# LayerNorm by pairs of batches, merged stores of the gate, earlier fetches for the mixing stage and an x store on two queues, in a fused delta-rule, gMLP and channel-mix kernel

## The chip, the cores and the metric

The kernel runs on one core of a Trainium2 chip. Its engines are TensorE (PE, with its weight loads as PEld), VectorE (DVE), ScalarE (ACT), GpSimd (POOL) and SyncE (SP), and each works through its own instructions in order. DMAs are issued here by SP and POOL, and after the change by ACT as well. The metric is the device time of one execution in microseconds (us). Three runs before the change took 823.33, 824.58 and 827.2 us.

## The reference

Three layers follow each other; 4 batches of 768 tokens, 8 heads of 48 features.

```python
k_n = k / (norm(k) + 1e-6)                       # layer 1: delta rule, token by token
for t in range(768):
    y[t]  = q[t] @ state
    state = state + beta[t] * outer(k_n[t], v[t] - k_n[t] @ state)
x = y with its heads side by side                # (4, 768, 384)

h = gelu_tanh(x @ w_in)                          # layer 2: gMLP, 1024 wide
u, v = h[..., :512], h[..., 512:]
v_n = (v - mean(v)) / sqrt(var(v) + 1e-6) * g_ln # over the 512 features
v_s = einsum('ts,bsd->btd', w_sg, v_n) + b_sg    # mixes all 768 tokens
x   = x + (u * v_s) @ w_out

xk, xr = blends of x and the x of the token before    # layer 3: channel mix
out = sigmoid(xr @ w_r) * (relu(xk @ w_k) ** 2 @ w_v)
```

All is float32; large products are made of three passes over values split in a high and a low part.

## The kernel before, in words

**The loop.** The tokens are cut into 12 steps of 64 (names with `s`); two steps are a group (`g`, 0 to 5). The 32 pairs of batch and head are handled in two halves `o`: batches 0 and 1, batches 2 and 3. Each step and half runs six stages (`st_rq`, `st_d0`, `st_l`, `st_d1`, `st_s`, `st_y`), the two halves three stages apart. PE's matmuls of a stage need the residual `r` that DVE makes (L426), and DVE's `r` needs the PE matmuls before it (L458, L488). For group g+1 DVE meanwhile inverts the triangular blocks (`solver`, L328 to L413, which ends with the transposed `DT` of L411).

**Layer 2 beside it.** When a group's x is done, `store_x` (L538) copies it by 8 DMAs for each half into `xT`; `x_split` (L558) makes its high and low part (`xh`, `xl`), and the products with `w_in` are put as *units* between the stages on PE: `v_units` (L588) for one batch each, `u_units` (L639) for two batches. `v_end` (L600) takes gelu of a v into one of four buffers `v`; `ln_steps` (L608) takes its statistics on DVE, and once the last batch is there, 4 small POOL operations (L622 to L625) make scale and shift for all four batches; `apply` (L628) then normalises each v in place on ACT and stores it to DRAM (`vn_d`, L634). A `v` buffer is free for the next group when that store has landed. In the last group the four operations are done for two batches at a time.

**Jobs.** The weights `w_out` and `w_k` come as float64 and are narrowed to high and low parts by jobs (`narrow`, L144): a load `raw`, ACT (L154), four DVE operations (L159 to L165), POOL (L167), ACT (L110), POOL (L113), and two stores (`put`, L192). `tick` (L789) starts jobs; from tick `LATE` on more of them.

**The order of the work.** In this stage the code is recorded in the order of `run`, `tick`, `fill` and `background` for PE, ACT, DVE and POOL, and their instructions stay in it. SP's instructions are placed by a scheduler.

**After the loop.** Lines 836 to 880 finish the last group's units and prepare the mixing with `w_sg`: `load_ws` loads a block of it (`wst`) and splits it into `ws0h`, `ws0l` or `ws1h`, `ws1l`; `load_v` loads a normalised v (`vst`) and splits it (`vh`, `vl`). `mix` and `project` (L923, L940) are layer 2's second half, `shift` and the last loop (L995 to L1044) layer 3.

Of the kernel before, what the change touches and what calls it, by code (L numbers as in the profile page):

```python
# [7 lines left out]
F32 = mybir.dt.float32  # L8
# [8 lines left out]
B, H, S, D = 4, 8, 768, 48  # L17
DM = 384
FF = 1024
HF = 512  # L20
P = 128
C = 64
NG = 6
# [13 lines left out]
RUN = (3, 1, 2)  # L37
SUMS = (0,)
EVERY = 12
LATE = 116  # L40
JLAG = 1
BUDGET = 1.4
UNITS = 6.1
GSTEP = 2
JS = 18
NT_ = (3, 3, 3)
LNW = 2
LAGX = 7
LAGU = 2
SHARE = ((1, 4, 1), (1, 3, 1), (2, 5, 1))  # L50
NRAW = 3
# [25 lines left out]
def fused_kernel(  # L77
# [17 lines left out]
    nc = tc.nc  # L95
    V, A, G, T = nc.vector, nc.scalar, nc.gpsimd, nc.tensor

    cp = ctx.enter_context(tc.tile_pool(name="cp", bufs=1))
    dp = ctx.enter_context(tc.tile_pool(name="dp", bufs=1, space=bass.MemoryType.DRAM))
    stg = ctx.enter_context(tc.tile_pool(name="stg", bufs=2))  # L100

    xT = cp.tile([P, B, 3, S + 1], F32, name="xT")
# [4 lines left out]
    def split(eng_hi, eng_lo, src, hi, lo):  # L107

        if eng_hi is A:
            A.activation(hi, src, AF.Copy)  # L110
        else:
            eng_hi.tensor_scalar(hi, src, 1.0, None, op0=ALU.mult)
        eng_lo.tensor_tensor(lo, src, hi.bitcast(F32), op=ALU.subtract)  # L113
# [69 lines left out]
    def scratch(dram, name, nblk, n, cw=CW, pool=stg):  # L183

        hi = dp.tile([nblk, P, n], F32, name=name + "_dh")
        lo = dp.tile([nblk, P, n], F32, name=name + "_dl")

        def job(i, j):
            parts = []
            yield from narrow(dram, i, j, None, None, cw, pool, parts=parts)  # L190

            def put():  # L192
                for d, x in zip((hi, lo), parts):
                    nc.sync.dma_start(out=d[i, :, j:j + cw], in_=x.bitcast(F32))

            yield 0, put

        return hi, lo, [lambda i=i, j=j: job(i, j) for i in range(nblk) for j in range(0, n, cw)]

# [7 lines left out]


    vn_d = dp.tile([B, NG, P, HF], F32, name="vn_d")
    u_d = dp.tile([B, 4, P, S], F32, name="u_d")  # L210
    wo_dh, wo_dl, jobs = scratch(w_out, "wo", 4, DM, DM // 2)
    wk_dh, wk_dl, j1 = scratch(w_k, "wk", 3, FF)
    jobs += j1
# [4 lines left out]
    with ExitStack() as at:  # L218
# [319 lines left out]
        def store_x(g, o, yst):  # L538
            ts_ = slice(1 + P * g, 1 + P * g + P)
            for h in range(2):  # L540
                for i in range(2):
                    nc.sync.dma_start(out=xT[D * h:D * h + D, 2 * o + i, :, ts_],  # L542
                                      in_=yst[64 * h:64 * h + D, 4 * i:4 * i + 3, :])
            for h, e, n, blk, row in ((0, 0, 32, 0, 96), (0, 32, 16, 1, 96),
                                      (1, 0, 16, 1, 112), (1, 16, 32, 2, 96)):
                nc.sync.dma_start(out=xT[row:row + n, 2 * o:2 * o + 2, blk, ts_],  # L546
                                  in_=yst[64 * h + e:64 * h + e + n, 3:8:4, :])


# [57 lines left out]

        def ln_steps(g, b, v):  # L608
            mv, vs = vstat[g]
            n = 2 if g == NG - 1 else B  # L610
            st6 = fp.tile([P, 6], F32, name="st6")
            V.bn_stats(out=st6, in_=v)
            yield 0.6
            V.bn_aggr(out=mv[:, b], in_=st6)
            yield 0.1
            if b % n == n - 1:
                b0 = b + 1 - n
                var = fp.tile([P, n], F32, name=f"var{n}")
                yield 1, None
                rs = fp.tile([P, n], F32, name=f"rs{n}")  # L620
                nm = fp.tile([P, n], F32, name=f"nm{n}")
                G.tensor_scalar(var, mv[:, b0:b + 1, 1], EPS, None, op0=ALU.add)  # L622
                G.tensor_scalar(nm, mv[:, b0:b + 1, 0], -1.0, None, op0=ALU.mult)
                G.tensor_tensor(rs, var, nhalf[:, :n], op=ALU.pow)
                G.tensor_tensor(nm, nm, rs, op=ALU.mult)  # L625
                yield 2, None

                def apply(i):  # L628
                    A.activation(vs[b0 + i], vs[b0 + i], AF.Identity, bias=nm[:, i:i + 1],
                                 scale=rs[:, i:i + 1])  # L630
                    if (b0 + i, g) == (0, NG - 1):
                        to_ring(0, g, vs[0])
                    else:
                        nc.sync.dma_start(out=vn_d[b0 + i, g], in_=vs[b0 + i])  # L634

                for i in range(n):
                    yield LNW, lambda i=i: apply(i)

        def u_units(g, o, e, xh, xl):  # L639
            def mm(d, c, i, first, last):  # L640
                if first and d == 0:
                    vstat["u"] = bank()[:].rearrange("p a b -> p (a b)")
                w, a = ((wu_hi, xh), (wu_lo, xh), (wu_hi, xl), (wu_lo, xl))[i]
                ds_ = slice((2 * e + d) * P, (2 * e + d) * P + P)
                T.matmul(vstat["u"][:, 2 * P * d:2 * P * d + 2 * P], lhsT=w[:, c, ds_],  # L645
                         rhs=a[:, c].rearrange("p b t -> p (b t)"), start=first, stop=last)
                if last and d:
                    ug = fp.tile([P, 2, 2, P], F32, name="ug")
                    A.activation(ug.rearrange("p d b t -> p (d b t)"), vstat["u"],
                                 AF.Gelu_apprx_tanh)  # L650
                    for k in range(2):
                        nc.sync.dma_start(
                            out=u_d[2 * o:2 * o + 2, 2 * e + k, :, P * g:P * g + P].rearrange(
                                "b p t -> p b t"), in_=ug[:, k])

            return (g, o), lambda: (steps(0.5, lambda *a: mm(0, *a), 1)
                                    + steps(0.5, lambda *a: mm(1, *a), 1))
# [67 lines left out]
        running = []  # L725
        jobs = in_jobs + jobs
# [34 lines left out]
        k = 0  # L761
# [27 lines left out]
        def tick():  # L789
            g, n = divmod(point[0], 24)  # L790
            point[1] = min(g, 1) + 1
            gg, nn = divmod(point[0] - GRAM0, 24)
            if nn == 0 and 0 <= gg and gg + 2 < NG:
                grams.extend(gram(gg + 2))
            if n == 0 and g + 1 < NG:
                streams.append([point[0] + SOLVE0, solver(g + 1), "solve"])
            late = point[0] >= LATE
            if jobs and len(running) < RUN[1 + late] and n % (4 if late else EVERY) == 0:
                start_job(LJ5 if late else LJ)
            background(BUDGET * (B0 if g == 0 else 1))  # L800
            while len(jobs) > n_rest and len(running) < RUN[0]:
                start_job()
            if grams and (point[0] - GRAM0) % GSTEP == 0:
                for _, f in grams.pop(0):
                    f()
            point[0] += 1
# [16 lines left out]
        while opened[0]:  # L823
# [8 lines left out]
    vr = vx.enter_context(tc.tile_pool(name="vr", bufs=9, side="right", reuse_waits="tile"))  # L832
    banks[0] = ps
    ws = [[wq.tile([P, 6, DM], F32R, name=f"ws{t}{x}", tag=f"w{t}{x}") for x in ("h", "l")]
          for t in range(2)]
    b_sb = wq.tile([P, S], F32, name="b_sb")
    nc.sync.dma_start(out=b_sb, in_=b_sg.partition_broadcast(P))

    def load_ws(t, i):
        wst = vr.tile([P, DM], F32, name="wst", bufs=3)  # L840
        nc.sync.dma_start(out=wst, in_=w_sg[i * P:(i + 1) * P, t * DM:t * DM + DM])
        split(A, V, wst, ws[t][0][:, i], ws[t][1][:, i])

    ring = {}

# [2 lines left out]
    def fetch_v(b, c):  # L848
        vsts[b, c] = vr.tile([P, HF], F32, name="vst", bufs=3)
        nc.sync.dma_start(out=vsts[b, c], in_=vn_d[b, c])  # L850

    def load_v(b, c):
        if (b, c) not in vsts:
            fetch_v(b, c)
        to_ring(b, c, vsts.pop((b, c)))

    def to_ring(b, c, vst):
        vh = vr.tile([P, HF], F32R, name="vh")
        vl = vr.tile([P, HF], F32R, name="vl")
        split(A, G if c % 3 else V, vst, vh, vl)  # L860
        ring[b, c] = (vh, vl)
# [3 lines left out]
        ahead += [lambda i=i: load_ws(0, i), lambda i=i: load_v(0, i)]  # L865
    ahead.append(lambda: load_ws(0, 5))
    for c in range(3):
        fetch_v(0, c)
    ahead += [lambda i=i: load_ws(1, i) for i in range(6)]
    while later or splits or units or streams or opened[0]:  # L870
        background(2)
        units.sort(key=lambda u: (u[0][0], u[2]))
        fill(5)
        point[0] += 1
        if ahead:
            ahead.pop(0)()
# [31 lines left out]
    us, gs = {}, {}  # L908

    def load_u(b, t):  # L910
        us[b, t] = mp.tile([P, 4, DM], F32, name="u", bufs=3)
        nc.sync.dma_start(out=us[b, t],
                          in_=u_d[b, :, :, t * DM:t * DM + DM].rearrange("d p t -> p d t"))

    def mix_mm(pt, b, t, d, c):
        ds_ = slice(d * P, d * P + P)
# [189 lines left out]
```

## Time and profile before

| | |
|---|---|
| three runs | 823.33, 824.58, 827.2 us |
| the profiled execution | 823.41 us, of which the trace spans 821.7 us |
| busy: PE, DVE, ACT, POOL | 724.4, 526.6, 361.1, 192.1 us |
| granted TensorE clock, mean | 0.956 of full speed |
| DMA packets, bytes | 84969, 89.20 MB, mean 109 GB/s |

The loop lasts to about 385 us of the span, the transition to 416 us, the mixing and projecting to 567 us and layer 3 to the end. A busy PE is not PE at its peak: the granted clock has two levels, and in the page's row of clocks a 9 is full speed. A row of the timeline gives start, duration, engine, line, operation, tiles, and in brackets how long the engine was idle before it and what ended that. `SPq` is the instant at which SP's queue issues a DMA.

### The profile page before, as it was taken

To read this page: it belongs to the slowest core of one execution; us is meant where nothing else is said; L and a number is where in the kernel's file an instruction comes from. 1 tells how busy PE (TensorE), PEld (TensorE's weight loads), DVE (VectorE), ACT (ScalarE), POOL (GpSimd) and SP (SyncE) were. 2 spreads that over 40 slices of the span, in tenths; PEclk is the share of its full clock that TensorE was granted. 3 is DMA by queue.
4 is the path that set the end of the run, shared out by engine and by line. 5 is a ranking of instruction groups with operands and counts; after the bars stand their busy time and mean duration, and the time that the engine had idled before them with its cause. 6 is when DMAs were issued, how large, how long until landed. Compare 5 with 4: busy or idle time off the path is not lost.

```text
span 821.7 us, 23659 instructions
## 1 busy us (share of the span) xinstructions
PE 724.4 (88%) x10126; PEld 657.4 (80%) x10126; DVE 526.6 (64%) x1087; ACT 361.1 (44%) x732; POOL 192.1 (23%) x226
## 2 busy tenths in 40 slices
PE   3388898969969969697779979999999999999998
PEld 3345676857857867486679969999999999999998
DVE  6989689668668679134349596738945645653432
ACT  2234455535635634555443333205744534542431
POOL 3254233323313412424323535111000000000000
PEclk9989999979979979889979989999999999999999
DMA  8313343344444434534598755308400000000000
GB/s 235 81 52 99 85 127 111 97 145 116 105 134 124 110 108 120 155 117 116 175 316 276 241 201 182 108 0 259 107 30 20 10 30 20 16 24 21 19 20 29
DMA packets 84969, 89.20 MB, mean 109 GB/s; under 512 B 25856, under 2 KB 68992, under 8 KB 84864
## 3 DMA queue, kind: packets, MB, share of 16 engines
q1 hardware_dynamic: 80128, 78.64, 31.7%
q0 software_dynamic: 4736, 9.04, 3.9%
q8 instruction: 79, 1.29, 0.7%
q14 instruction: 26, 0.21, 0.1%
HBM read 56.86 MB, written 26.08 MB: 101 GB/s over the span
## 4 chain that ended last, share of the span: by engine, by line
PE 63%; DVE 11%; DMA 7%; SPq 5%; ACT 3%; issue 2%; POOL 1%; ACTq 0%; DVEq 0%; POOLq 0%
PE ms L141 34%; PE ms L920 8%; PE ms L645 4%; PE ms L593 3%; PE rk L434 3%; PE ms L522 3%; DVE tmp L325 2%; PE rk L488 2%; SPq L546 2%; DMA vn_d<-v 2%; SPq L542 2%; PE rk L458 2%; PE ms L686 2%; PE sps L508 1%; DMA wk_dh<-raw 1%
## 5 line engine op out<-in xcount | busy, mean ns | idle before, releaser
L426 DVE TENSOR_TENSOR r<-vk,rk 128x384 f32<-128x384 f32 x40 | 22.0, 551 | 83.4 <-PE rk L488 53.2
L167 POOL TENSOR_TENSOR na<-na,raw 128x256 int32<-128x256 int32 (+2 forms) x43 | 36.7, 853 | 126.2 <-DVE na L165 83.0
L141 PE MATMUL ms<-wvh,sh 128*128 128x384 f32 x192 | 64.9, 338 | 0.0
L141 PE MATMUL ms<-wvl,sh 128*128 128x384 f32 x192 | 64.9, 338 | 0.0
L141 PE MATMUL ms<-wvh,sl 128*128 128x384 f32 x192 | 64.8, 338 | 0.0
L141 PE MATMUL ms<-xm_hi,wkh 128*128 128x384 f32 x192 | 64.1, 334 | 0.0
L141 PE MATMUL ms<-xm_lo,wkh 128*128 128x384 f32 x192 | 64.1, 334 | 0.0
L141 PE MATMUL ms<-xm_hi,wkl 128*128 128x384 f32 x192 | 64.1, 334 | 0.0
L474 POOL TENSOR_SCALAR_AFFINE_SELECT SQ<-SQ 64x512 f32<-64x512 f32 x48 | 36.4, 757 | 93.8 <-ACT SQ L473 92.2
L522 PE MATMUL ms<-SQ 128*64 128x64 f32 x768 | 30.9, 240 | 28.9 <-ACT v L602 28.9
L522 PEld LDWEIGHTS ms<-SQ 128*64 128x64 f32 x768 | 27.5, 152 | 34.6 <-ACT v L602 30.1
L113 DVE TENSOR_TENSOR sl<-r,sh 128x384 fp32r<-128x384 f32 x64 | 35.6, 557 | 30.2 <-ACT sh L110 30.2
L110 ACT ACTIVATE sh<-r 128x384 fp32r<-128x384 f32 x64 | 33.5, 524 | 36.0 <-DVE r L1026 36.0
L434 PEld LDWEIGHTS rk<-r,DT 32*32 32x32 f32 x1536 | 35.3, 105 | 13.2 <-issue 3.7
L434 PE MATMUL rk<-r,DT 32*32 32x48 f32 x1536 | 41.7, 202 | 3.6 <-DVE r L426 2.3
L920 PE MATMUL ms<-ws0h,vh 128*128 128x384 f32 x96 | 33.1, 345 | 11.3 <-ACT ws0h L110 11.2
L304 PE MATMUL ms<-kT 64*32 64x64 f32 (+1 forms) x896 | 31.8, 227 | 12.5 <-issue 12.5
L1026 DVE TENSOR_TENSOR r<-r 128x384 f32<-128x384 f32 x64 | 35.3, 552 | 9.7 <-ACT r L1025 9.7
L1042 DVE TENSOR_TENSOR ob<-th,ms 128x384 f32<-128x384 f32 x24 | 13.2, 552 | 43.4 <-PE ms L141 43.4
L499 ACT ACTIVATE SQ<-rk 64x384 f32<-64x384 f32 x48 | 23.3, 485 | 39.9 <-PE rk L434 38.9
L302 PE MATMUL ms<-kT 64*32 64x64 f32 (+1 forms) x896 | 31.3, 228 | 10.6 <-DMA kT<-in_kt_d_dram 6.8
L1025 ACT ACTIVATE r<-ms 128x384 f32<-128x384 f32 x64 | 30.7, 480 | 20.4 <-PE ms L141 19.7
(160 smaller groups left out, 2266.9 us busy)
## 6 DMA issues: line engine op xcount, KB each, us to landing
kT<-in_kt_d_dram SPq DMA_DIRECT2D x12, 512.0 KB, 4.4
u_d<-ug SPq DMA_DIRECT2D x48, 128.0 KB, 1.9
u<-u_d SPq DMA_DIRECT2D x8, 768.0 KB, 6.6
vn_d<-v SPq DMA_DIRECT2D x23, 256.0 KB, 3.8
vst<-vn_d SPq DMA_DIRECT2D x23, 256.0 KB, 3.2
SQ<-in_q_d_dram SPq DMA_DIRECT2D x48, 96.0 KB, 3.2
vk<-in_vk_dram SPq DMA_DIRECT2D x24, 192.0 KB, 3.4
vk<-in_vk_dram SPq DMA_DIRECT2D x12, 384.0 KB, 4.0
```

The lines of the kernel that those rows point to most:

```text
L110: A.activation(hi, src, AF.Copy)
L113: eng_lo.tensor_tensor(lo, src, hi.bitcast(F32), op=ALU.subtract)
L141: T.matmul(pt, lhsT=a, rhs=b, start=(i == 0), stop=(i == n - 1))
L167: G.tensor_tensor(a.bitcast(I32), a.bitcast(I32), w_lo.bitcast(I32), op=ALU.add)
L302: T.matmul(gps[r:r + 32, p, c0:c1], lhsT=t[r:r + 64, u, 0:32], rhs=t[r:r + 64, u, c0:c1], start=True, stop=True)
L304: T.matmul(gps[r + 32:r + 64, p, c0:c1], lhsT=t[r:r + 64, u, 32:64], rhs=vw2(t, r, 64, u * C + 32, [(0, (c1 - c0) // 32), (1, 32)]), start ...
L434: T.matmul(RQs[o][b0:b0 + 32, p, 0:D], lhsT=DT[b0:b0 + 32, u0 + p, :], rhs=t[b0:b0 + 32, p, :], start=True, stop=True, skip_group_check=True)
L474: G.affine_select(out=pt, in_=pt, pattern=[[0, 8], [1, C]], compare_op=ALU.is_gt, fill=0.0, base=0, channel_multiplier=-1)
L522: T.matmul(yps[b0:b0 + 64, p, :], lhsT=cur[h][:, p, 0:64], rhs=cur[h][:, p, D:], start=True, stop=True)
L645: T.matmul(vstat["u"][:, 2 * P * d:2 * P * d + 2 * P], lhsT=w[:, c, ds_], rhs=a[:, c].rearrange("p b t -> p (b t)"), start=first, stop=last)
L920: T.matmul(pt[:, :DM], lhsT=v[:, ds_], rhs=w[:, c], start=(c == 0 and i == 0), stop=(c == 5 and i == 2))
L1026: V.tensor_tensor(r, r, r, op=ALU.mult)
```

## The change

1. **LayerNorm by pairs.** `n = 2` for all groups: scale and shift are made when batches 0 and 1 are there, and again for 2 and 3. `LNW` (ticks between two `apply`) is 1 and not 2.
2. **Gate in one store.** `u_d` gets another layout, so that one DMA stores what two did (48 become 24); `load_u` uses two DMAs where it used one (8 become 16).
3. **Fetches for the mixing.** The blocks `wst` are fetched three ahead of the split that uses them, the first three before `b_sb`, and `vst` of chunks 3 and 4 as soon as chunks 0 and 1 are split.
4. **Last x.** In the last group 4 of the 8 DMAs of each half are issued by ACT.
5. **Jobs.** More jobs from tick 100 on (not 116), a start at every second tick (not every fourth); a job's stores are issued two ticks later (`PUT`). `LAGX`, the ticks from a group's x store to its split, is 6 and not 7.

```diff
-LATE = 116
+LATE = 100
+PUT = 2
-LNW = 2
-LAGX = 7
+LNW = 1
+LAGX = 6
@@ scratch.job
-            yield 0, put
+            yield PUT, put
@@
-    u_d = dp.tile([B, 4, P, S], F32, name="u_d")
+    u_d = dp.tile([2, 2, P, 2, 2, S], F32, name="u_d")
@@ store_x
-                    nc.sync.dma_start(out=xT[D * h:D * h + D, 2 * o + i, :, ts_],
+                    (nc.scalar if g == NG - 1 and i else nc.sync).dma_start(out=xT[D * h:D * h + D, 2 * o + i, :, ts_],
...
-                nc.sync.dma_start(out=xT[row:row + n, 2 * o:2 * o + 2, blk, ts_],
+                (nc.scalar if g == NG - 1 and h else nc.sync).dma_start(
+                                  out=xT[row:row + n, 2 * o:2 * o + 2, blk, ts_],
@@ ln_steps
-            n = 2 if g == NG - 1 else B
+            n = 2
@@ u_units
-                    for k in range(2):
-                        nc.sync.dma_start(
-                            out=u_d[2 * o:2 * o + 2, 2 * e + k, :, P * g:P * g + P].rearrange(
-                                "b p t -> p b t"), in_=ug[:, k])
+                    nc.sync.dma_start(
+                        out=u_d[o, e, :, :, :, P * g:P * g + P], in_=ug)
@@ tick
-            if jobs and len(running) < RUN[1 + late] and n % (4 if late else EVERY) == 0:
+            if jobs and len(running) < RUN[1 + late] and n % (2 if late else EVERY) == 0:
@@ before the mixing
-    nc.sync.dma_start(out=b_sb, in_=b_sg.partition_broadcast(P))
+    wsts = {}
+    def fetch_ws(j):
+        if j < 12:
+            t, i = divmod(j, 6)
+            wsts[j] = vr.tile([P, DM], F32, name="wst", bufs=3)
+            nc.sync.dma_start(out=wsts[j], in_=w_sg[i * P:(i + 1) * P, t * DM:t * DM + DM])
 
     def load_ws(t, i):
-        wst = vr.tile([P, DM], F32, name="wst", bufs=3)
-        nc.sync.dma_start(out=wst, in_=w_sg[i * P:(i + 1) * P, t * DM:t * DM + DM])
-        split(A, V, wst, ws[t][0][:, i], ws[t][1][:, i])
+        split(A, V, wsts.pop(6 * t + i), ws[t][0][:, i], ws[t][1][:, i])
+        fetch_ws(6 * t + i + 3)
@@ load_v
         to_ring(b, c, vsts.pop((b, c)))
+        if b == 0 and c < 2:
+            fetch_v(0, c + 3)
@@
     for c in range(3):
+        fetch_ws(c)
         fetch_v(0, c)
     ahead += [lambda i=i: load_ws(1, i) for i in range(6)]
+    nc.sync.dma_start(out=b_sb, in_=b_sg.partition_broadcast(P))
@@ load_u
-        nc.sync.dma_start(out=us[b, t],
-                          in_=u_d[b, :, :, t * DM:t * DM + DM].rearrange("d p t -> p d t"))
+        for e in range(2):
+            nc.sync.dma_start(out=us[b, t][:, 2 * e:2 * e + 2],
+                              in_=u_d[b // 2, e, :, :, b % 2, t * DM:t * DM + DM])
```

PE has the same instructions in the same order before and after. What moves stands on the other engines. A few lines below the change are numbered 1 to 11 higher after it (L634 before is L636 after, L629 is L631, L110 is L111).

First the queue of SP, where the x of group 1 and its normalised v are stored. Before, at the end of the group (`xT<-yst` is half 1 of the x store, `vn_d<-v` the v store of batch 0, then of batches 1 and 2):

```order
L251 DMA SQ_117<-in_q_d_dram 48x8x64
L251 DMA SQ_118<-in_q_d_dram 48x8x64
L542 DMA xT<-yst 48x3x128 x4
L546 DMA xT<-yst 32x2x128
L546 DMA xT<-yst 16x2x128 x2
L546 DMA xT<-yst 32x2x128
L246 DMA vk<-in_vk_dram 128x768
L634 DMA vn_d<-v 128x512
L239 DMA kT_94<-in_kt_d_dram 128x1024
L634 DMA vn_d<-v 128x512 x2
```

And after, where the two v stores that stand first are batches 0 and 1, and the x store below them is half 0 of group 1:

```order
L252 DMA SQ_115<-in_q_d_dram 48x8x64
L252 DMA SQ_116<-in_q_d_dram 48x8x64
L636 DMA vn_d<-v 128x512
L653 DMA u_d<-ug 512x1x128
L240 DMA kT_97<-in_kt_d_dram 128x1024
L636 DMA vn_d<-v 128x512
L195 DMA wo_dh<-raw 128x192
L195 DMA wo_dl<-na 128x192
L151 DMA raw<-in_w_out_dram 128x384
L252 DMA SQ_113<-in_q_d_dram 48x8x64
L252 DMA SQ_114<-in_q_d_dram 48x8x64
L543 DMA xT<-yst 48x3x128 x4
```

The stores of batches 0 and 1 have moved from behind both halves of the group's x store to a place ahead of them; those of batches 2 and 3 follow one before and one after half 1 of it.

Second, ACT in the transition, from the last x (`yst`, half 1) to the split of x. Before:

```order
L649 ACTIVATE ug<-ms 128x512
L154 ACTIVATE raw<-raw 128x256
L527 ACTIVATE yst<-ms 128x8x64
L629 ACTIVATE v<-v,nm_6293,rs_6292 128x512
L110 ACTIVATE xh<-xT 128x768
L629 ACTIVATE v<-v,nm_6293,rs_6292 128x512 x2
L110 ACTIVATE raw<-na 128x256
```

And after, with the DMAs that ACT now issues:

```order
L651 ACTIVATE ug<-ms 128x512
L528 ACTIVATE yst<-ms 128x8x64
L543 DMA xT<-yst 48x3x128 x2
L547 DMA xT<-yst 16x2x128
L547 DMA xT<-yst 32x2x128
L631 ACTIVATE v<-v,nm_6310,rs_6309 128x512
L111 ACTIVATE xh<-xT 128x768
L111 ACTIVATE raw<-na 128x256
```

Four DMA issues have come between `yst` and the first `xh`.

Third, ACT at the end of the transition, where the mixing's first operands are split. Before:

```order
L629 ACTIVATE v<-v,nm_6626,rs_6625 128x512
L154 ACTIVATE raw<-raw 128x256
L649 ACTIVATE ug<-ms 128x512
L110 ACTIVATE vh<-vst 128x512 x2
L110 ACTIVATE raw<-na 128x256
L110 ACTIVATE vh<-vst 128x512
L110 ACTIVATE ws0h<-wst 128x384 x3
L110 ACTIVATE vh<-vst 128x512 x2
```

And after:

```order
L155 ACTIVATE raw<-raw 128x256
L651 ACTIVATE ug<-ms 128x512
L111 ACTIVATE raw<-na 128x256
L604 ACTIVATE v<-ms 128x512 x2
L631 ACTIVATE v<-v,nm_6641,rs_6640 128x512
L651 ACTIVATE ug<-ms 128x512
L631 ACTIVATE v<-v,nm_6641,rs_6640 128x512
L111 ACTIVATE ws0h<-wst 128x384
L651 ACTIVATE ug<-ms 128x512
L111 ACTIVATE vh<-vst 128x512
```

The first split of `wst` stands right behind the last normalisation, and the last job's two steps (`raw`) have moved from the mixing's first splits to a place ahead of the last two gelus.

## Rows read from the trace of the kernel before

**Rows 1.** Waits of PE, whole trace: us in total, times, longest
```profile
PE ms L522 <- ACT v L602: 28.9, 6, 7.4
PE ms L920 <- ACT ws0h L110: 11.2, 1, 11.2
PE ms L593 <- ACT GL L311: 3.9, 6, 0.7
```
**Rows 2.** Timeline of ACT, groups 1 and 2: start, us, operation
```profile
161.23 0.80 ACT L629 ACTIVATE v<-v,nm,rs 128x512 f32<-128x512 f32 x1
...
175.10 0.60 ACT L602 ACTIVATE v<-ms 128x512 f32<-128x512 f32 x1 [6.11 <-DMA vn_d<-v]
```
**Rows 3.** Timeline of SP's queue, same stretch
```profile
164.65 3.21 SPq L542 DMA_DIRECT2D xT<-yst  x4
...
167.90 2.53 SPq L546 DMA_DIRECT2D xT<-yst  x4
...
171.16 0.37 SPq L634 DMA_DIRECT2D vn_d<-v  x1
```
**Rows 4.** Timeline of DVE, the residual r at one place of groups 1 to 5
```profile
112.98 0.55 DVE L426 TENSOR_TENSOR r<-vk,rk 128x384 f32<-128x384 f32 x1
...
165.42 0.54 DVE L426 TENSOR_TENSOR r<-vk,rk 128x384 f32<-128x384 f32 x1
...
284.30 0.54 DVE L426 TENSOR_TENSOR r<-vk,rk 128x384 f32<-128x384 f32 x1
...
298.01 0.56 DVE L426 TENSOR_TENSOR r<-vk,rk 128x384 f32<-128x384 f32 x1 [5.09 <-PE rk L488]
...
352.32 0.55 DVE L426 TENSOR_TENSOR r<-vk,rk 128x384 f32<-128x384 f32 x1 [13.52 <-PE rk L488]
```
**Rows 5.** Timeline of PE: end of group 4's solver, then group 5's stall
```profile
325.12 0.87 PE L434 MATMUL rk<-r,DT 32*32 32x48 f32 x32 [0.99 <-DVE r L426]
...
348.81 1.98 PE L522 MATMUL ms<-SQ 128*64 128x64 f32 x32 [7.41 <-ACT v L602]
```
**Rows 6.** Windows: stretch, us, busy PE PEld DVE ACT POOL, PEclk, DMA share, GB/s
```profile
349.00:357.00 8.00, 8.00 (x136) 7.15 (x138) 2.56 (x7) 3.25 (x6) 1.66 (x3) 0.61 0.39 136
```
**Rows 7.** Timeline of PE in the transition
```profile
386.16 1.65 PE L593 MATMUL ms<-wiv_hi,xh 128*128 128x512 f32 x3 [3.60 <-ACT xh L110]
...
399.57 0.84 PE L593 MATMUL ms<-wiv_hi,xl 128*128 128x512 f32 x3
...
415.89 0.69 PE L920 MATMUL ms<-ws0h,vh 128*128 128x384 f32 x1 [11.17 <-ACT ws0h L110]
```
**Rows 8.** Chain that ended last: start, us, what
```profile
407.74 7.55 DMA wst<-in_w_sg_dram
```
**Rows 9.** Timeline of DVE, a w_k job's first and last operation
```profile
358.70 0.28 DVE L159 TENSOR_SCALAR na<-raw 128x256 uint32<-128x256 uint32 x1
...
359.67 0.42 DVE L165 SCALAR_TENSOR_TENSOR na<-raw,na 128x256 uint32<-128x256 uint32 x1
```
**Rows 10.** Timeline of DVE, the last batch's statistics
```profile
403.57 0.69 DVE L612 BATCH_NORM_STATS2 st<-v 128x6 f32<-128x512 f32 x1 [2.33 <-ACT v L602]
```
**Rows 11.** Timeline of POOL, one LayerNorm pair of group 5
```profile
400.71 0.24 POOL L622 TENSOR_SCALAR var<-mv 128x2 f32<-128x2 f32 x1
...
402.01 0.19 POOL L625 TENSOR_TENSOR nm<-nm,rs 128x2 f32<-128x2 f32 x1
```
**Rows 12.** A DMA group: count, KB each, us from issue to landing
```profile
raw<-in_w_k_dram SPq DMA_DIRECT2D x12, 256.0 KB, 3.1
```
**Rows 13.** Timeline of DVE in group 1's solver
```profile
121.92 0.69 DVE L325 TENSOR_TENSOR tmp<-NT,Yt 128x512 f32<-128x512 f32 x1
...
123.37 1.33 DVE L325 TENSOR_TENSOR tmp<-Dm,NT 128x512 f32<-128x512 f32 x1
```
**Rows 14.** Timeline of POOL beside rows 13
```profile
122.32 1.83 POOL L113 TENSOR_TENSOR xl<-xT,xh 128x768 fp32r<-128x768 f32 x1 [7.10 <-DMA SQ<-in_q_d_dram]
```
**Rows 15.** Waits of ACT: us in total, times, longest
```profile
ACT raw L110 <- POOL na L167: 39.6, 22, 3.8
```

## The prediction, made before the result

> **What bounds the kernel now.** I read the busy slices of the page first: PE is busy nearly without a gap in the last third and only in part in the loop, so what can be won lies before the mixing. Then the waits of PE. One line leads them: the matmuls of L522, the head of a group's outputs, wait 28.9 us in six places for the gelu `v` of L602 [rows 1], and the first mixing product waits 11.2 us for `ws0h`. The next, for the eviction `GL`, is 3.9 us in six places.
>
> The timeline of ACT and SP's queue tell where the 28.9 us come from. In group 1 the first `v` was normalised at 161.23. The next gelu, which wants that buffer again, begins at 175.10 after 6.11 us idle, released by a store of `vn_d` [rows 2]. That store was issued only at 171.16, because the eight x stores stand ahead of it on SP from 164.65 on [rows 3]. ACT works in order, PE's outputs need a PSUM tile behind that gelu, and the whole loop stops. So the stall is a queue's order and not the work of an engine.
>
> What does DVE do meanwhile? I compare one place of each group, the residual `r` [rows 4]. Group 1, whose buffers are fresh and which has no such stall, takes 165.42 − 112.98 = 52.44 us; groups 2 and 3 together take 284.30 − 165.42 = 118.88, which is 14.00 more than two times 52.44. In group 4 DVE has idled 5.09 us before this `r`, and later PE waits for `r` again, 0.99 us at 325.12 [rows 5]: beside the solver DVE is nearly the bound, so it wins back only what it idled. In group 5 there is no solver, DVE has idled 13.52 us, and PE is the bound: the 7.41 us at 348.81 are PE's own. After that stall the granted clock is 0.61 of full speed for 8.00 us [rows 6], a mixture of the two levels, which costs 8.00 × 0.39 = 3.1 us.
>
> In the transition PE waits 3.60 us for the split of x and 11.17 us for `ws0h`, the latter until 415.89 [rows 7]. The chain ends in a fetch of `wst`, issued at 407.74 and 7.55 us long [rows 8], so data that could have been asked for sooner.
>
> **The change part by part.** *LayerNorm by pairs.* The order shows the stores of batches 0 and 1 ahead of the x stores. By the rows above they are issued some 25 us sooner, longer than any landing here, while batches 2 and 3, stored later than before, are needed later too (the gelus come batch by batch, half a group apart). The stall should go in groups 2 to 5. What is late next is DVE's `r` in groups 2 to 4, and nothing nearer than PE's own work in group 5. So I price groups 2 and 3 by group 1's period, −14.0; group 4 by DVE's idle time, −5.1, of which the one w_k job that now starts there takes back its four DVE operations, 358.70 to 360.09, +1.4 [rows 9]; group 5 by the stall and the clock behind it, −7.4 − 3.1 = −10.5. Together −28.2. The price: normalising batches 0 and 1 now stands before the evictions for which PE's L593 waits (3.9 us in six places already [rows 1]); one 0.80 us normalisation [rows 2] in groups 1 to 3 makes +2.4. `LNW` and `LAGX` move ACT and POOL work by a tick inside this cover; nothing if the cover holds, and if it doesn't, the same 0.80 again.
>
> *Jobs.* More jobs before the mixing means fewer beside it; they load DVE and ACT when DVE has idled 13.5 us, so beyond the 1.4 above I cost them at nothing (rival D is what they cost if that is wrong). Their stores wait two ticks, on SP, which nothing is behind that PE needs at once.
>
> *Last x on two queues.* ACT now issues four DMAs between the last `yst` and the first split `xh`, for which PE already waits. Before shows no DMA issue on ACT. On SP four of the one kind take 3.21 and four of the other 2.53 [rows 3]; two of each are 2.9. Ends: nothing, if issuing is cheap on ACT or the earlier landing pays for it, and 3.6, one whole wait of this place again. I take 2.9, the price on SP being the only one shown.
>
> *Fetches ahead.* `wst` no longer waits for POOL, and `ws0h` stands right behind the last normalisation. The way there: PE's last `v` product ends at 399.57 + 0.84 [rows 7], 2.9 later now, 403.3; its gelu 0.6 [rows 2]; statistics 0.69 and 0.2 for the aggregate [rows 10], 404.8 (in before they began at 403.57 after waiting for a gelu that stood behind a normalisation; it stands ahead now); POOL's four operations 400.71 to 402.20, 1.5 [rows 11], 406.3; then on ACT two normalisations, two gelus and the first two splits, 2 × 0.8 + 4 × 0.6, 410.3. Even the slow landing of 7.55 is over by then if `wst` is asked for at 402. So PE goes on at about 410.3 and not 415.89: −5.6, the 2.9 included. Ends: nothing, if the late jobs, all of which now stand ahead of those gelus, hold ACT as long as the fetch did; −11.2 if the wait went away whole.
>
> *Gate in one store, gate loads in two.* 24 fewer stores take work from SP, which in the loop waits rather than works. The loads are eight more issues: 8 × 0.37 [rows 3] is 3.0 us if they bear on PE, and one landing of 3.1 us [rows 12] is the most that earlier blocks could win in the mixing. I take 0, since the first wait is the only long one of PE there.
>
> Sum: −28.2 + 2.4 − 5.6 = −31.4, from 823.41 to 792.0. The three runs have their median 1.17 above the profiled execution, so about 793.
>
> One rule speaks against the change. In group 1's solver the product of L325 took 1.33 us where its like took 0.69 just before [rows 13], and POOL split x beside it, 1.83 us from 122.32 on [rows 14]. The Trainium skill, GPSIMD Engine Reference, section Specifications, says that POOL's way to SBUF is shared with VectorE and contended when a DVE instruction has two SBUF inputs, as this one has; the trace agrees. LayerNorm by pairs adds POOL's four operations once more in each of groups 1 to 4. By that rule they could hold the solver by their own length, 4 × 1.5 = 6.0 us, and the time would be 799, inside the forecast's own range; by the rows they are operations on two columns, where the split had 768, and I add nothing.
>
> **The rivals.**
> A. PE gets the whole stall back: DVE is not late, since its idle time before `r` moves along. Then −28.9, and the clock stays up after four stalls and not one, −4 × 3.1 = −12.4, with the transition's −5.6: 823.41 − 46.9 + 1.2 = 778. For it: 28.9 us is what the waits say. Against it: the 0.99 us for which PE waits on `r` as soon as group 4's stall is made good, and the 14.0 us that bound groups 2 and 3.
> B. Other waits eat more: groups 2 to 4 win the 5.09 of group 4 each, less 1.4 and 2.4, so 11.5, group 5 its 7.4 without the clock, the transition nothing: 823.41 − 18.9 + 1.2 = 806.
> C. The change doesn't do what it says: the stores of batches 2 and 3, now the late ones, hold ACT in place of the others. Then only the transition gains, 5.6 less 2.4: 821. Against it: those gelus come half a group later.
> D. Slower: jobs hold ACT. Twelve w_k jobs [rows 12] run in the tightest part; each first step stands in ACT's order behind a landing of 3.1, and its second behind POOL, 39.6 / 22 = 1.8 [rows 15]. If PE stood behind ACT each time, 12 × 4.9 = 58.8, and 823.4 − 31.4 + 58.8 + 1.2 = 852. It turns slower from 31.4 / 12 = 2.6 us a job on. Against it: the same jobs wait in the kernel before without a line of PE that names them.
>
> **How the numbers follow.** Forecast 0.63, A 0.13, B 0.16, C 0.03, D 0.05. The likeliest one's own range comes from its bounds: below, 5.6 more in the transition and 3.1 in the mixing, 784; above, 5.6 and 3.0, 802. For 8 in 10 it takes in most of A and of B: 775 to 809. About 0.5%, 4.1 us, is what a measurement of this kernel can tell from no change. Forecast, A and B are faster by more than that, 0.92; C is within it, 0.03; D slower, 0.05.
>
> **What would show it.** The wait of L522 for `v` should be gone from groups 2 to 5, the places of rows 4 some 52 us apart up to group 3, and waits of PE for `r` should appear there; if they don't, A. PE's clock should stay at full speed where rows 6 show 0.61. PE's first mixing product should start 5 to 6 us sooner after the last product with `w_in`; ACT's DMA issues should take about 0.7 us each between `yst` and `xh`. New idle time of ACT before the jobs' steps, with PE's wait behind it, would show D; a wait of L522 for `v` with a store of batch 2 or 3 as its releaser, C.

## The result, and the profile after

The changed kernel took 801.35 us (median of four runs, 800.34 to 802.09) against 825.89 before; the ratio is 0.9706, with a 95% interval of 0.9676 to 0.9736. The forecast was 793, range 775 to 809: faster, as forecast, by some 24 us where 31 had been worked out. The profiled execution took 801.47 us, to be set against 792.0 of the sum; its trace spans 799.8 us, before 821.7.

First the waits of PE, after (us in total, times, longest), which answer to [rows 1]:

```profile
...
PE rk L435 <- DVE r L427: 9.5, 6, 2.4
...
PE ms L595 <- ACT GL L312: 6.0, 6, 1.4
...
PE ms L595 <- ACT xh L111: 4.9, 1, 4.9
PE ms L931 <- ACT vh L111: 4.3, 1, 4.3
PE ms L523 <- ACT ug L651: 3.4, 1, 3.4
...
PE ms L523 <- ACT v L604: 1.0, 1, 1.0
```

Of the 28.9 us for `v` 1.0 is left. The wait for DVE's `r`, 2.3 us in all before, is now the longest that a tile ends (above it stands only the 12.1 us of `issue`, 12.5 before). New is one for a gelu `ug`, which no term of the sum had.

The stall's cause as SP's queue shows it after, up to the end of group 1, beside [rows 3]. The four `vn_d` are batches 0 to 3 of one group:

```profile
134.42 0.56 SPq L636 DMA_DIRECT2D vn_d<-v  x1
...
140.96 0.33 SPq L636 DMA_DIRECT2D vn_d<-v  x1
...
160.10 0.33 SPq L636 DMA_DIRECT2D vn_d<-v  x1
...
163.96 2.58 SPq L543 DMA_DIRECT2D xT<-yst  x4
166.58 3.42 SPq L547 DMA_DIRECT2D xT<-yst  x4
...
170.74 0.37 SPq L636 DMA_DIRECT2D vn_d<-v  x1
```

and ACT in the same stretch, where [rows 2] had a gelu that idled 6.11 us for a store:

```profile
169.07 0.60 ACT L604 ACTIVATE v<-ms 128x512 f32<-128x512 f32 x1
...
173.24 0.60 ACT L604 ACTIVATE v<-ms 128x512 f32<-128x512 f32 x1 [1.52 <-PE ms L595]
```

Batch 0, whose store went out at 171.16 before, is now stored at 134.42, some 37 us sooner, where "some 25" had been estimated. A store of `vn_d` still stands behind the x stores, at 170.74, but it is that of batch 3, and no gelu waits for it. The first gelu of the next group begins at 169.07 with no wait worth a mark, the second waits for its own product.

DVE's `r` at the places of [rows 4]:

```profile
113.19 0.55 DVE L427 TENSOR_TENSOR r<-vk,rk 128x384 f32<-128x384 f32 x1
...
166.00 0.54 DVE L427 TENSOR_TENSOR r<-vk,rk 128x384 f32<-128x384 f32 x1
...
273.99 0.54 DVE L427 TENSOR_TENSOR r<-vk,rk 128x384 f32<-128x384 f32 x1
...
282.55 0.55 DVE L427 TENSOR_TENSOR r<-vk,rk 128x384 f32<-128x384 f32 x1
...
327.52 0.55 DVE L427 TENSOR_TENSOR r<-vk,rk 128x384 f32<-128x384 f32 x1 [7.50 <-PE rk L489]
```

Group 1 takes 52.81 us, 0.37 more than before; groups 2 and 3 take 107.99, which was 118.88. DVE's idle time before the fourth `r` (5.09) is gone. That DVE is late there now is one row of PE:

```profile
288.23 0.87 PE L435 MATMUL rk<-r,DT 32*32 32x48 f32 x32 [2.44 <-DVE r L427]
```

To see where the rest went, I cut the spans at four instructions that all traces have: the third of the forty `r` of L426, the last `r`, the first product of L593 with the last group's x (half 0, for which PE waits), the first mixing product (L920) and the first product with `w_k`. Stage lengths in us, each the difference of two starts in one trace:

| kernel | loop | to last x | to mixing | mixing | layer 3 |
|---|---|---|---|---|---|
| before | 263.1 | 10.1 | 29.7 | 163.2 | 242.6 |
| after | 236.9 | 15.6 | 23.0 | 168.5 | 242.6 |
| difference | −26.2 | +5.5 | −6.7 | +5.3 | 0 |

(From 113.0 on to the span's end; what lies ahead is the same within 0.2. The mixing is taken with its projections, up to 579.1 us before; 567, as said at the top, is the end of the last mixing product, and projections follow it.) So the loop gave what was forecast, and the stages behind it together cost 4.1 us where 5.6 of gain were forecast. Over the loop the granted clock is 0.92 before and 0.99 after, and 1.00 in the 8 us from 324 on, the place of [rows 6], as the prediction's signs had it.

The second stage is seen on ACT, from the last group's `yst` of half 0 to that of half 1 and the first split, after:

```profile
349.17 0.60 ACT L528 ACTIVATE yst<-ms 128x512 f32<-128x512 f32 x1 [0.25 <-PE ms L523]
349.80 1.57 ACTq L543 DMA_DIRECT2D xT<-yst  x2
351.41 1.38 ACTq L547 DMA_DIRECT2D xT<-yst  x2
...
357.76 0.42 ACT L111 ACTIVATE raw<-na 128x256 fp32r<-128x256 f32 x1 [1.63 <-POOL na L168]
358.08 0.58 ACT L651 ACTIVATE ug<-ms 128x512 f32<-128x512 f32 x1
...
360.82 0.60 ACT L528 ACTIVATE yst<-ms 128x512 f32<-128x512 f32 x1 [0.97 <-PE ms L523]
361.45 1.28 ACTq L543 DMA_DIRECT2D xT<-yst  x2
362.77 1.26 ACTq L547 DMA_DIRECT2D xT<-yst  x2
364.08 0.81 ACT L631 ACTIVATE v<-v,nm,rs 128x512 f32<-128x512 f32 x1 [2.66 <-DMA xT<-yst]
364.80 0.83 ACT L111 ACTIVATE xh<-xT 128x768 fp32r<-128x768 f32 x1
```

`ACTq` is an issue of a DMA by ACT. Four take 2.95 us of ACT's time, and four more 2.54 (the 2.66 "for xT" of the row at 364.08 are those issues, not a landing). In between a job's step waits 1.63 us for POOL, and the gelu `ug`, for which PE waits 3.4 us at 358.81, stands behind it.

The fourth stage, the mixing, can be followed product by product: its 864 products stand in the same order in every trace. Start of some of them, in us from the first product of the mixing, with two of the experiments below:

| kernel | 109th | 325th | 361st | 433rd | 469th | first with `w_k` |
|---|---|---|---|---|---|---|
| before | 22.5 | 60.8 | 75.7 | 88.3 | 94.5 | 163.2 |
| after | 28.6 | 66.1 | 76.1 | 88.6 | 99.8 | 168.5 |
| fetches as before | 21.5 | 62.7 | 74.5 | 88.2 | 94.5 | 163.2 |
| pairs alone | 21.5 | 61.9 | 76.4 | 90.9 | 98.1 | 166.7 |

At first the changed kernel falls 6.1 us behind. Windows of 4 us there, after (us, busy PE, PEld, DVE, ACT, POOL, then the granted clock, DMA share, GB/s):

```profile
400.00:404.00 4.00, 3.31 (x19) 3.19 (x19) 2.09 (x3) 1.28 (x4) 0.76 (x1) 1.00 0.81 256
404.00:408.00 4.00, 3.22 (x18) 2.62 (x16) 2.33 (x5) 1.80 (x4) 0.00 (x0) 1.00 0.92 294
408.00:412.00 4.00, 2.85 (x9) 1.63 (x8) 3.88 (x9) 1.57 (x4) 0.00 (x0) 0.74 1.05 342
412.00:416.00 4.00, 4.00 (x14) 4.00 (x13) 3.09 (x7) 0.99 (x2) 0.00 (x0) 0.50 1.05 390
```

PE, which started sooner, is idle 0.7 to 1.2 us in each of three windows, at DMA shares of 0.81 to 1.05, and its clock goes to the lower of its two levels for the window of 412 to 416. But this is not what the stage lost in the end: up to the 361st product nearly all of it is made good. Before, PE waits there 4.6 us in six places for `gh` and `gl`, and its clock falls too. The longest of these waits, and the windows:

```profile
484.77 0.63 PE L141 MATMUL ms<-gh,wo_hi 128*128 128x384 f32 x1 [2.16 <-ACT gh L110]
```

```profile
484.00:488.00 4.00, 2.22 (x4) 1.02 (x4) 4.00 (x8) 1.25 (x3) 1.65 (x2) 0.61 0.31 104
488.00:492.00 4.00, 3.27 (x12) 3.16 (x12) 3.29 (x6) 1.57 (x3) 1.49 (x2) 0.54 0.98 331
```

After, the same places cost 2.4 us of waits, at full clock. The 5.3 us come between the 433rd and the 469th product, the first of batch 2, where PE before never waits. After, on PE, DVE and in windows:

```profile
478.80 0.45 PE L931 MATMUL ms<-ws0h,vl 128*128 128x384 f32 x1 [1.03 <-DVE vl L114]
...
484.37 0.44 PE L142 MATMUL ms<-gl,wo_hi 128*128 128x384 f32 x1 [1.83 <-DVE gl L114]
```

```profile
481.45 1.33 DVE L162 TENSOR_SCALAR na<-na 128x384 f32<-128x384 f32 x1
482.81 1.03 DVE L164 TENSOR_SCALAR na<-na 128x384 uint32<-128x384 uint32 x1
483.77 0.54 DVE L114 TENSOR_TENSOR gl<-w,gh 128x384 fp32r<-128x384 f32 x1
```

```profile
480.00:484.00 4.00, 2.54 (x15) 2.22 (x13) 3.16 (x5) 1.15 (x3) 3.63 (x3) 1.00 0.18 68
484.00:488.00 4.00, 3.63 (x13) 3.63 (x14) 1.26 (x3) 1.04 (x2) 1.04 (x2) 0.63 0.85 256
```

Two waits make 2.9 us, and the lower clock in the second window 4 × 0.37 = 1.5. The `gl` that PE waits for stands on DVE behind two operations of a `w_v` job, which took 1.33 and 1.03 us here and 0.35 each at 472.50 and 473.23; POOL works on `vl` from 479.58 to 482.56. Over the whole mixing PE is idle 8.1 us where it was 5.6, and the mean granted clock is 0.96 against 0.97.

### The profile page after: what moved, and what is told of

Same layout as the page of the kernel before. It is cut to its first block, busy times and chain, and to the rows that moved or that the text cites. A ratio compares the mean times of both kernels' runs of the same rounds, so it can differ in the third digit from the quotient of the medians.

```text
span 799.8 us, 23669 instructions
## 1 busy us (share of the span) xinstructions
PE 719.3 (90%) x10126; PEld 652.8 (82%) x10126; DVE 524.5 (66%) x1087; ACT 360.6 (45%) x732; POOL 201.4 (25%) x246
## 4 chain that ended last, share of the span: by engine, by line
PE 58%; DVE 14%; DMA 8%; ACT 4%; issue 3%; POOL 3%; SPq 3%; ACTq 0%; DVEq 0%; POOLq 0%
PE ms L142 34%; PE ms L931 6%; PE ms L647 3%; PE ms L595 3%; DVE tmp L326 3%; PE rk L435 3%; PE ms L523 2%; DMA raw<-in_w_v_dram 2%; POOL na L168 1%; PE sps L509 1%; PE ms L686 1%; PE rk L489 1%; SPq L547 1%; DMA vst<-vn_d 1%; PE ms L303 1%
## 5 line engine op out<-in xcount | busy, mean ns | idle before, releaser
L435 PEld LDWEIGHTS rk<-r,DT 32*32 32x32 f32 x1536 | 35.3, 105 | 20.6 <-DVE r L427 10.6
L111 ACT ACTIVATE sh<-r 128x384 fp32r<-128x384 f32 x64 | 33.5, 524 | 35.7 <-DVE r L1037 35.7
L305 PE MATMUL ms<-kT 64*32 64x64 f32 (+1 forms) x896 | 31.6, 229 | 12.1 <-issue 12.1
L595 PE MATMUL ms<-wiv_hi,xh 128*128 128x512 f32 x72 | 30.2, 439 | 12.2 <-ACT GL L312 6.0
L500 ACT ACTIVATE SQ<-rk 64x384 f32<-64x384 f32 x48 | 23.3, 485 | 35.8 <-PE rk L435 33.3
L647 PE MATMUL ms<-xl,wiu_hi 128*128 128x256 f32 x144 | 39.3, 300 | 0.0
L111 ACT ACTIVATE gh<-w 128x384 fp32r<-128x384 f32 x32 | 16.6, 521 | 50.3 <-DVE w L946 50.3
```

The costliest lines, as they stand in the source:

```text
L305: T.matmul(gps[r + 32:r + 64, p, c0:c1], lhsT=t[r:r + 64, u, 32:64], rhs=vw2(t, r, 64, u * C + 32, [(0, (c1 - c0) // 32), (1, 32)]), start ...
L435: T.matmul(RQs[o][b0:b0 + 32, p, 0:D], lhsT=DT[b0:b0 + 32, u0 + p, :], rhs=t[b0:b0 + 32, p, :], start=True, stop=True, skip_group_check=True)
L595: T.matmul(vstat[g, b], lhsT=a[:, c], rhs=w[:, c], start=first, stop=last)
```

## The experiments

The theory: a `v` buffer held by a late store made the stall, and pairs cure it whole; the rest of the change wins at the mixing's first wait and pays for it in ACT's order. The rival: the parts need each other. Medians are set against the kernel before run on the same chip; the interval is that of the ratio.

**Pairs alone**, on the kernel before:

```diff
-            n = 2 if g == NG - 1 else B
+            n = 2
```

> The kernel before with one edit: LayerNorm by pairs in every group. Theory (the loop's stall was a v buffer held by a store that stood behind the x stores, and pairs alone cure it): the loop wins some 26 us as in the changed kernel, the transition and the mixing stay as before, so about 826 - 26 = 800 us; and since the changed kernel gave back about 4 us behind the loop, even 797 to 800. Rival (the gain needs the shorter steps and the other jobs as well): less than half of it, 813 us or more, with waits of L522 for v left over.

Measured: 801.93 us, ratio 0.9685 (0.9639 to 0.9731). Waits of PE:

```profile
PE rk L434 <- DVE r L426: 9.8, 6, 2.3
PE ms L920 <- ACT ws0h L110: 9.7, 1, 9.7
...
PE ms L593 <- ACT GL L311: 6.0, 6, 1.4
```

One line gives the whole gain: its loop takes 237.0 us, and 2.6 us are left of the wait for `v`. The rest of the change adds nothing that can be measured on top. That the mixing stays as before did not come: it takes 166.7, and at the first products of batch 2 PE waits for `vh` (1.78) and `vl` (0.49).

**More buffers in place of pairs**, on the kernel before:

```diff
-            v = fp.tile([P, HF], F32, name="v", bufs=4)
+            v = fp.tile([P, HF], F32, name="v", bufs=6)
```

> The kernel before with one edit: 6 buffers for v and not 4, LayerNorm over four batches as before. Theory (buffers): the next group's first two gelus no longer wait for the stores, so the same 26 us go: about 800 us, no wait of L522 for v. Rival (pairs win by what they do on POOL and ACT, not by the buffers): 815 us or more.

Measured: 801.35 us, ratio 0.9667 (0.9615 to 0.9718); the loop takes 238.1. Waits of PE:

```profile
PE rk L434 <- DVE r L426: 9.8, 6, 2.3
...
PE ms L522 <- ACT v L602: 4.0, 6, 1.4
PE ms L593 <- ACT GL L311: 3.9, 6, 0.7
```

With LayerNorm over four batches untouched, two more buffers do the same, though 4.0 us of waits for `v` are left where none was expected, and PE then waits for `r` exactly as long as with pairs. So it is the buffer that stalled, and DVE that bounds the loop next. The wait for `GL` stays at 3.9 us here and is 6.0 with pairs: that is the price of pairs, 2.1.

**The last x on SP alone**, in the changed kernel:

```diff
-                    (nc.scalar if g == NG - 1 and i else nc.sync).dma_start(out=xT[D * h:D * h + D, 2 * o + i, :, ts_],
+                    nc.sync.dma_start(out=xT[D * h:D * h + D, 2 * o + i, :, ts_],
...
-                (nc.scalar if g == NG - 1 and h else nc.sync).dma_start(
+                nc.sync.dma_start(
```

> The changed kernel with the last x stored by SP alone, as before. Theory (the four issues on ACT, 2.6 us of its time, stand between yst and xh and cost PE that): PE's wait of 4.9 us for xh falls to about 2, time 801.4 - 3 = 798 us. Rival (the second queue pays for itself by an earlier landing): the wait stays or grows, 801 to 804 us.

Measured: 798.55 us, ratio 0.966 (0.9629 to 0.9692). The first product for the last x:

```profile
362.43 0.80 PE L595 MATMUL ms<-wiv_hi,xh 128*128 128x512 f32 x1 [2.13 <-ACT xh L111]
```

The wait is 2.13 and not 4.9, and the stage to the last x 10.9 and not 15.6 us. The second queue doesn't pay for itself. By time alone the interval still overlaps that of the changed kernel; it is the stage that shows it.

**Jobs as before**, in the changed kernel:

```diff
-LATE = 100
-PUT = 2
+LATE = 116
+PUT = 0
...
-            if jobs and len(running) < RUN[1 + late] and n % (2 if late else EVERY) == 0:
+            if jobs and len(running) < RUN[1 + late] and n % (4 if late else EVERY) == 0:
```

> The changed kernel with jobs started as before (from tick 116, every fourth tick, stores at once). Theory (jobs' steps in ACT's order hold the last gelus: the 3.4 us wait of L523 for ug and the half clock of 352 to 376 us follow from them): 801.4 - 6 = 795 us, and the clock of the transition higher than 0.79. Rival (jobs that leave the transition return in the mixing and cost as much there): 800 to 803 us, and the mixing is longer by what the transition wins.

Measured: 799.75 us, ratio 0.9666 (0.9634 to 0.9699). The wait for `ug` falls to 0.83 us, but the one for `xh` grows:

```profile
364.59 0.79 PE L595 MATMUL ms<-wiv_hi,xh 128*128 128x512 f32 x1 [6.24 <-ACT xh L111]
```

The stage takes 13.6 us, 2.0 less, and the expected 6 did not come: with the issues on ACT left in, most of the wait only moved to the next product. The granted clock over the 24 us of the transition is 0.86 (351 to 375), 0.79 in the changed kernel (352 to 376), higher as expected, and the mixing takes 165.2, 3.3 less than there, against the rival. By time alone this run can't be told from the changed kernel.

**Fetches as before**, in the changed kernel:

```diff
+    nc.sync.dma_start(out=b_sb, in_=b_sg.partition_broadcast(P))
...
-        split(A, V, wsts.pop(6 * t + i), ws[t][0][:, i], ws[t][1][:, i])
-        fetch_ws(6 * t + i + 3)
+        wst = vr.tile([P, DM], F32, name="wst", bufs=3)
+        nc.sync.dma_start(out=wst, in_=w_sg[i * P:(i + 1) * P, t * DM:t * DM + DM])
+        split(A, V, wst, ws[t][0][:, i], ws[t][1][:, i])
...
-        if b == 0 and c < 2:
-            fetch_v(0, c + 3)
...
-        fetch_ws(c)
...
-    nc.sync.dma_start(out=b_sb, in_=b_sg.partition_broadcast(P))
```

> The changed kernel with the fetches for the mixing as before. Theory (fetching ahead is what cut the first wait of the mixing): PE's wait for its first operand there goes from 4.3 back to about 9.5 us, and the time from 801.4 to 805. Rival (what is won at the mixing's start is lost inside it, where the blocks were not late): the mixing starts later and ends as before, 800 to 802.

Measured: 804.17 us, ratio 0.9727 (0.9702 to 0.9752). The mixing's first product, and then a window over its first 22.3 us:

```profile
395.16 0.69 PE L922 MATMUL ms<-ws0h,vh 128*128 128x384 f32 x1 [10.46 <-ACT ws0h L111]
```

```profile
395.20:417.50 22.30, 22.30 (x113) 21.90 (x114) 13.50 (x25) 9.09 (x17) 2.72 (x3) 0.88 0.95 318
```

The stage to the mixing takes 29.6 us, as before the change, and the mixing 163.2, as before too: PE starts later and in these 22.3 us never waits, though its clock is at 0.88. So fetching ahead wins 6.6 us in front of the mixing and loses 5.3 of them in it, in profiles (802.64 us against 801.47); the medians differ by 3 to 4 us. Both theories were half right.

**The gate as before**, in the changed kernel (two stores and, not shown, one load):

```diff
-    u_d = dp.tile([2, 2, P, 2, 2, S], F32, name="u_d")
+    u_d = dp.tile([B, 4, P, S], F32, name="u_d")
...
-                    nc.sync.dma_start(
-                        out=u_d[o, e, :, :, :, P * g:P * g + P], in_=ug)
+                    for k in range(2):
+                        nc.sync.dma_start(
+                            out=u_d[2 * o:2 * o + 2, 2 * e + k, :, P * g:P * g + P].rearrange(
+                                "b p t -> p b t"), in_=ug[:, k])
```

> The changed kernel with two stores of the gate and one load, as before. Theory (both hidden): 801.4 within 1.5 us. Rival (sixteen loads of half the size hold the queue in the mixing, where the changed kernel lost 5 us): 797 to 799, and the mixing shorter by that.

Measured: 799.2 us, ratio 0.9677 (0.9655 to 0.9698), an interval that overlaps that of the changed kernel; the mixing takes 167.0. It doesn't tell the two apart.

**x and jobs both as before**, the two edits above together in the changed kernel:

```diff
-LATE = 100
+LATE = 116
...
-                    (nc.scalar if g == NG - 1 and i else nc.sync).dma_start(out=xT[D * h:D * h + D, 2 * o + i, :, ts_],
+                    nc.sync.dma_start(out=xT[D * h:D * h + D, 2 * o + i, :, ts_],
```

> The changed kernel with both the last x on SP alone and the jobs as before. Theory (two separate prices in ACT's order, 2.8 and 1.6 us by the runs with one of them undone): they add up, 801.4 - 4.4 = 797 us. Rival (both are the same wait of ACT): 798.5 to 800, no better than the x alone.

Measured: 795.62 us, ratio 0.963 (0.961 to 0.965). The same two places of PE:

```profile
360.25 1.31 PE L595 MATMUL ms<-wiv_hi,xh 128*128 128x512 f32 x3 [3.28 <-ACT xh L111]
...
385.14 0.69 PE L931 MATMUL ms<-ws0h,vh 128*128 128x384 f32 x1 [4.27 <-ACT vh L111]
```

The stage to the last x is 9.7 us, 0.3 below that of the kernel before, so these two edits account for all of what it had grown: x 4.7 and jobs 2.0 taken away singly, 5.9 together.

**Pairs and fetches alone**, on the kernel before:

```diff
-            n = 2 if g == NG - 1 else B
+            n = 2
...
-        split(A, V, wst, ws[t][0][:, i], ws[t][1][:, i])
+        split(A, V, wsts.pop(6 * t + i), ws[t][0][:, i], ws[t][1][:, i])
+        fetch_ws(6 * t + i + 3)
```

(and the other lines of the fetches as in the change)

> The kernel before with LayerNorm by pairs and the fetches ahead, nothing else. Theory (these two carry all that is won, the rest is hidden or costs): as the run with x and jobs undone, 796 to 798 us. Rival (the rest of the change pays too): 800 us or more.

Measured: 795.29 us, ratio 0.9625 (0.9597 to 0.9654). The first product of its mixing waits less than in the changed kernel:

```profile
386.47 0.57 PE L930 MATMUL ms<-ws0h,vh 128*128 128x384 f32 x1 [3.72 <-ACT vh L110]
```

Two of the change's five parts carry all of the gain. This is the fastest kernel of the study, and the one before it has the same time.

**Buffers and fetches**, that kernel with `bufs=6` in place of the pairs:

```diff
-            n = 2
+            n = 2 if g == NG - 1 else B
...
-            v = fp.tile([P, HF], F32, name="v", bufs=4)
+            v = fp.tile([P, HF], F32, name="v", bufs=6)
```

> The kernel before with 6 buffers for v in place of the pairs, and the fetches ahead. Theory (buffers and pairs cure the same wait, and pairs alone pay some 2 us where L593 waits for GL): 2 us faster than pairs with fetches, 793 us. Rival (the remaining waits of L522 for v, 4.0 us in six places with 6 buffers, eat that): 795 to 797.

Measured: 797.1 us, ratio 0.9643 (0.9619 to 0.9668): the 2 us of `GL` (3.9 here) bring no gain. 4.0 us of waits for `v` stand against them, and the mixing takes 169.2, the longest of all.

**Pairs, fetches and the merged gate**, the layout edit above, with its one store and two loads, added to the pairs and fetches:

```diff
-    u_d = dp.tile([B, 4, P, S], F32, name="u_d")
+    u_d = dp.tile([2, 2, P, 2, 2, S], F32, name="u_d")
```

> Pairs and fetches as in the run e8_pairs_fetch, with the gate's merged store and split loads added. Theory (hidden): 795.3 within 1.5 us. Rival (the run with the gate as before was 2 us faster than the changed kernel, so the merged form costs 2): 797 to 798.

Measured: 797.61 us, ratio 0.9643 (0.9615 to 0.9671). Twice now the merged gate stands some 2 us on the slow side, and twice within the intervals. Against a cost stands the run with x and jobs as before, which has the merged gate too and took 795.62. Whether it costs anything stays open. That run differs from this one only in `LNW` and `LAGX`, so these show no effect beyond the intervals either.

**The changed kernel again** (no edit):

> The changed kernel itself once more, so that these two stand beside it on one chip: 801.4 within 1.5 us, 5 to 6 above pairs with fetches alone. If it came out below 798, the difference between it and that run would lie in the chips and not in the kernels.

Measured: 800.04 us, ratio 0.9675 (0.9646 to 0.9703), 4.75 above the median of pairs with fetches, within what was expected of it and just under the 5 to 6 of difference. Its profile has the stages of the first one (237.5, 15.6, 23.3, 166.5). Its interval lies above that of pairs with fetches but for 0.0008, where the two ends overlap.

## Why the prediction was right, and where it wasn't

*LayerNorm by pairs: right.* −28.2 + 2.4 = −25.8 was forecast for the loop, and −26.2 measured. Inside, group 1 paid 0.4 where 0.8 had been set, groups 2 and 3 gave 10.9 where 14.0 less twice 0.8 had been set, and groups 4 and 5 gave 15.8 up to the last `r` where 5.1 − 1.4 + 10.5 made 14.2. That the sum fits so closely is luck: misses of 1.5 and 1.6 cancel. The gain grew from 15.6 to 26.2 us between the `r` at 325.89 and the one at 357.41 of before, over the stall of group 5: 10.6, against −7.4 − 3.1 for stall and clock. The price on `GL` was set at 2.4 and is 2.1. That buffers were the cause, and not what pairs do elsewhere, was argued there and is shown by the run with six buffers. DVE was the next bound, as [rows 4, 5] had said, and so rival A fell: PE waits 9.5 us for `r`. So did C: no store of batch 2 or 3 holds a gelu for long, 1.0 us is left in all. B had the loop too low, but its "the transition nothing" was nearer than the forecast's 5.6.

*The rule on POOL's shared way to SBUF* (the Trainium skill, GPSIMD Engine Reference, section Specifications) would have had the doubled POOL operations cost up to 6.0 us. The loop takes 237.0 us with pairs and 238.1 with four batches at a time and more buffers, and the solver's products of L325 take 49.7 us in all in both; no such cost shows.

*Last x on two queues: a step that failed, by size.* The issue price was right, 2.9 against 2.54 us for the four between `yst` and `xh`. What the sum left out is the other four, issued after the first of the two `yst`: they push ACT's later work back by 2.95 us, behind them a job's step and the gelu `ug` that PE waits for. The stage cost 5.5 us and not 2.9, more than the bound of 3.6, and the run with x on SP alone takes 4.7 of that away (3.9 with the jobs as before).

*Jobs: "I cost them at nothing" was wrong by 1 to 2 us* (13.6 against 9.7 is x alone, 10.9 against 9.7 jobs alone). It is rival D's mechanism, at one place and not twelve.

*Fetches ahead: the wait went, by less than forecast.* Set against the price on x, they were worth −8.5 in the sum (−5.6 with 2.9 taken in); 6.7 were measured up to the mixing's first product. With the 5.5 in front of it the transition as a whole gave 1.2 us where 5.6 had been forecast.

*The mixing at nothing, with 3.1 and 3.0 as its bounds, was the step that failed most:* it grew by 5.3 us. "The first wait is the only long one of PE there" overlooked that before, too, PE waited 2.16 us for `gh` at 484.77, with a clock of 0.61 and 0.54 behind it. The 6.1 us that the changed kernel loses at the start, where PE comes sooner and waits for its operands, are made good at that place; the 5.3 are lost at batch 2, where PE waits 1.03 us for `vl` and 1.83 for `gl`, both of DVE, and the clock falls behind that. The clock alone is not the cause: over the mixing it is 0.96 after, 0.97 before and 0.95 with the fetches as before, which took 163.2. PE's idle time there differs more: 8.1, 5.6 and 4.6 us. Why DVE comes late at batch 2 is not shown by a run of its own. Nor is it the fetches by themselves: pairs alone wait at the same place and take 166.7. The mixing stays at 163.2 to 163.3 only in the kernel before, with six buffers alone and with the fetches as before in the changed kernel; in all other runs it takes 165.2 to 169.2. Which part of an edit brings that stays open.

So the loop carried the forecast, and 801.35 us lies in the range because the range had room for the misses behind the loop: the transition came out near its bound of nothing, and the mixing beyond its bound of 3.0.

*Gate*: hidden, or 2 us dear; not settled.

## What to carry to other kernels

When an engine waits for a buffer, look in the queue at what stands ahead of the store that frees it; one earlier store, or two more buffers, can be worth more than any work saved. Price a DMA issue on a compute engine as that engine's time at every place where it is issued, and count what stands behind it in order. A first wait that is removed shows the next limit, so the stage behind it can't be set at nothing because its other waits were short before. And follow a stage by its products to its end before you name what it lost: a loss at its start can be made good further on.

## What the hardware showed that was not expected

DMA issues by ACT took 0.63 to 0.79 us each (2.54 and 2.95 for four), much like SP's 0.63 to 0.80 [rows 3]. And PE's granted clock fell to 0.50 in the window from 412 to 416 us after three windows in which PE was busy 83, 80 and 71 per cent, the third of them at 0.74 already; no single wait in them was above 0.82 us. It came back, and in the changed kernel it fell again behind waits of 1.03 and 1.83 us, to 0.63 from 484 to 488.
